# Mirroring more of a symmetric score matrix in a gated attention unit followed by a mixture of experts

## The chip, the cores and the metric

The kernel runs on one core of one Trainium2 chip. The metric is the device time of one execution in microseconds (us). Before the change it is 883.23 us, the median of three runs (883.2 to 883.38). Engines are called by their names or as the profile has them: PE is TensorE's matmuls, PEld its weight loads, DVE VectorE, ACT ScalarE, POOL GpSimd, SP SyncE, which here only issues DMAs.

## What is computed

The reference has two stages. With B = 8 sequences of S = 2816 rows, D = 256 and 64 columns of z:

```python
def _attn_ref(u, v, z):
    scores = (1.0 / S) * np.matmul(z, z.transpose(0, 2, 1))
    attn = np.maximum(scores, 0.0) ** 2
    out = np.matmul(attn, v)
    return u * out

def _moe_ref(x, w_gate, w1_dense, w2_dense, w1, w2):   # x: the 22528 rows of the first stage
    y_dense = np.maximum(x @ w1_dense, 0.0) @ w2_dense
    logits = x @ w_gate
    expert_idx = np.argmax(logits, axis=1)              # one of 8 experts for each row
    probs = softmax(logits)
    for e in range(8):
        rows = expert_idx == e
        y_moe[rows] = probs[rows, e][:, None] * (np.maximum(x[rows] @ w1[e], 0.0) @ w2[e])
    return y_dense + y_moe
```

Since the scores are z times its own transpose, each sequence's attention matrix is symmetric: the block of keys k and queries q is the transpose of the block of keys q and queries k.

## The kernel before

**Blocks and groups.** A sequence is cut into 22 blocks of 128 rows. The queries of a sequence are worked off in six groups of 2, 4, 4, 4, 4 and 4 blocks (line 268). For each group `n` there is a buffer `A[n]` in SBUF with the squared scores of all 22 key blocks against the group's query blocks, in bf16. There are three such buffers, so group `n` takes the buffer of group `n - 3`; `open_group` (line 353) hands it out.

**Scores.** One call of `scores` (line 375) issues two matmuls on the two halves of TensorE's rows (64 columns of z each; the turned z, `zT`, holds z twice) and fills one pair of PSUM banks with two key blocks by four query blocks, 1024 numbers a partition. `relu` (line 397) then offers two passes, each to ScalarE or VectorE (the second of the first two groups also to GpSimd): relu and scale from PSUM to `r` (lines 405 and 407), and the square from `r` to `A[n]` (lines 418 and 420).

**Mirrored scores before.** For a group two back in the same sequence (`far[n]`, line 346) the scores are not computed again: a DMA transpose on SP's queue (line 468, in `far_steps`) writes the blocks of `A[n - 2]`, turned, into `A[n]` where they would have been. So `left[n]`, the list of score calls still to be issued for a group, leaves those keys out. The four transposes of a sequence are put into a list `turning` when the group that they read begins, and each is issued at one of a few places inside the multiplication (line 586), when the plan holds the source to be complete.

**Products.** `av(n, i, between)` (line 553) multiplies two query blocks of a group with `v`: two passes over the 22 key blocks, on each half of the rows one matmul per key block (line 579), 88 matmuls in all into one pair of banks. In the first two blocks of a group the first pass takes the keys in the order in which the plan expects them (`key_at`). Between the matmuls `fill` (line 483) issues score calls of this group, the next, or the one after it (`ahead`, line 495), when a pair of banks is free. Between the two passes `swap_rows` (line 531) issues a tiny matmul (`touch`, line 527) and two score calls, or two touches if no score may be computed ahead.

**After the products.** `gate_x` (line 602) multiplies with u on VectorE (line 606), which frees the output banks, and has SP turn the result (`xT`, line 608) for the expert logits. u comes in on SP's queue (`load_u`, line 141) four blocks ahead. Then each block is routed, and its rows are scattered by expert into a table in DRAM (`scatter`, line 717, on GpSimd's queue).

**The order.** The order of TensorE, ScalarE, VectorE and SP is written out by the program while it is built. The planner keeps a clock `now`, times at which each engine is free, and estimates of durations; `offer` and `run` hand the passes to the engine that ends first. Work tied to a block is registered with `at` and `soon`: `soon(t, ...)` puts it on VectorE at block `t` (counted over all sequences). In this way z of the next sequence is loaded at block 0 of each sequence (`load_z`, line 103, GpSimd's queue), and turned at blocks 5 and 6 (`turn_z`, line 108: a VectorE copy that doubles z, line 113, and a DMA transpose on SP's queue, line 116). v of the next sequence is loaded in eight parts at blocks 13 to 18. The weights of the second stage go into `wall` (8 experts, 2048 columns each), three loads a sequence at blocks 15, 18 and 21, from sequence 1 on.

**Second stage.** When the attention is done, the rows come back by expert in tiles of 256 or 128 (`fetch`), are multiplied with the dense weights and the expert's (`up`, `down`, lines 936 and 944), and scattered to the output (line 962). The change does not touch it.

Of the kernel before, what the change touches and what calls it, by code (L numbers as in the profile page):

```python
# [15 lines left out]
P = 128  # L16
# [3 lines left out]
def kernel(  # L20
# [13 lines left out]
    B, S, D = u.shape  # L34
    dq = z.shape[2]
    E = moe_w_gate.shape[1]
    F = moe_w1_dense.shape[1]
    N = B * S
    assert D == 256 and dq == 64 and F == 512 and E == 8 and S % (2 * P) == 0
    nK = S // P  # L40
# [19 lines left out]
    WD = 2 * F + 4 * D  # L60
# [47 lines left out]
    def turn_z(b, k0, k1):  # L108

        if k0 == 0:  # L110
            zn_of[b] = zpool.tile([P, nK, 2, dq], BF, name="zn", bufs=1)
            zT_of[b] = zpool.tile([P, nK, P], BF, name="zT")
        nc.vector.tensor_copy(
            zn_of[b][:, k0:k1, :, :],
            z_of[b][:, k0:k1, :].unsqueeze(2).to_broadcast([P, k1 - k0, 2, dq]))
        nc.sync.dma_start_transpose(
            out=zT_of[b][:, k0:k1, :],
            in_=zn_of[b][:, k0:k1].rearrange("p k h d -> p (k h d)"))
        if k1 == nK:
            z_there.add(b)  # L120

# [11 lines left out]
    now = [0.0]  # L133
# [4 lines left out]

    z_of, zn_of, zT_of, v_of, ut_of, xT_of, lg_of, rs = {}, {}, {}, {}, {}, {}, {}, {}

    def load_u(g, gate=False):
        ut = aw.tile([P, 2, D], F32, name="ut", bufs=3)
        if gate:
            nc.vector.memset(ut[:, 0, 0:1], 0.0)
        b, i = divmod(g, nK)
        nc.sync.dma_start(out=ut[:], in_=uf[:, b, i:i + 2, :])
        ut_of[g] = ut[:]


# [114 lines left out]
    A = {}  # L264
    groups = []
# [75 lines left out]
        run(now[0])  # L341


    left, far, key_at = {}, {}, {}
    for n, (b, i0, w) in enumerate(groups):
        far[n] = [m for m in (n - 2,) if m >= 0
                  if groups[m][0] == b]
        turned = {k for m in far[n] for k in range(groups[m][1], groups[m][1] + groups[m][2])}
        ks = [k for k in range(0, nK, 2) if k not in turned]

        left[n] = [tuple(ks[x:x + 4 // w]) for x in range(0, len(ks), 4 // w)]
# [88 lines left out]
        ts = [key_at.get((m, k)) for k in range(i0, i0 + w)]  # L440
        return None if None in ts else max(ts)

    def turned_to(a, n):

        _, j0, wj = groups[a]
        w = groups[n][2]
        flat = A[n].rearrange("p k c -> p (k c)")
        return flat[:, j0 * w * P:(j0 + wj) * w * P]

    def block(n, k, c):  # L450

        _, i0, w = groups[n]
        for a in far[n]:
            _, j0, wj = groups[a]
            if j0 <= k < j0 + wj:
                x = c * wj + k - j0
                return turned_to(a, n)[:, x * P:(x + 1) * P]
        return A[n][:, k, c * P:(c + 1) * P]

    def far_steps(a):  # L460

        _, j0, wj = groups[a]

        def step(n):
            _, i0, w = groups[n]
            assert a + 1 in A
            open_group(n)
            nc.sync.dma_start_transpose(
                out=turned_to(a, n).rearrange("p (x c) -> p x c", c=P),
                in_=A[a][:, i0:i0 + w, :].rearrange("p k c -> p (k c)"))  # L470
            turn_at[0] = now[0] + 0.17 * w * wj
            read_at[a] = now[0] + 1.5 + 0.19 * w * wj
            for j in range(wj):
                key_at[n, j0 + j] = now[0] + 7.0

        return [(a, lambda n=n: step(n), n) for n in (a + 2,) if a in far.get(n, [])]

    turning = []
    turn_at = [0.0]
    read_at = {}  # L480
    jobs = []

# [70 lines left out]
    def av(n, i, between):  # L553
        b, i0, w = groups[n]
        if i == i0:
            turning.extend(far_steps(n))
        keep[0] = 0
        if n == 0 and i == i0:

            fill(n)  # L560
            need(n, 0)
        until(lambda: pairs[0][0] if pairs else None)
        ox = take_pair()
        o = banks(ox, "o")
        for p in range(2):
            rest = list(range(nK))
            for x in range(nK):
                k = rest[0]
                if i == i0 and p == 0:

                    k = min(rest, key=lambda k: (max(key_at.get((n, k), 9e9), v_at(n, k)), k))
                    need(n, k)
                rest.remove(k)
                if n == 0 and i == i0 and p == 0 and x in (12, 14, 16):
                    load_u(2 * (x - 12) // 2, gate=True)
                for h in range(2):
                    r = slice(h * dq, (h + 1) * dq)
                    j = p ^ h
                    nc.tensor.matmul(out=o[:, j, 0:D], lhsT=block(n, k, i + j - i0)[r],  # L579
                                     rhs=v_of[b][r, k, :], start=(p == 0 and x == 0),  # L580
                                     stop=(p == 1 and x == nK - 1))
                pe(0.1092)
                keep[0] = 2 - p if x >= nK - 12 else 0
                if x % 2 == 1 and x < nK - 1:
                    fill(n)
                if x in (3, 10, 17)[1 - p:] and turning and turn_at[0] <= now[0]:
                    t = can_turn(turning[0][2], turning[0][0])
                    if t is not None and t <= now[0] and turning[0][0] + 1 in A:
                        turning.pop(0)[1]()
            if p == 0:  # L590
                swap_rows(n)
                between()

        def done(t):
            give_pair(t + 0.1, ox)

        g = b * nK + i
        offer(now[0] + 0.2, 0, {"dve": (0.63, lambda eng: gate_x(g, o))}, done)
        keep[0] = 0


    def gate_x(g, o):
        g0 = g % (2 * G)
        x = pays[:, g0:g0 + 2, 0:D]
        assert g + 1 < 2 * G or (g - 2 * G in placed and g + 1 - 2 * G in placed)
        nc.vector.tensor_mul(x, o[:, :, 0:D], ut_of.pop(g))  # L606
        xT = aw.tile([P, 5, P], BF, name="xT", bufs=8)
        nc.sync.dma_start_transpose(
            out=xT[:], in_=pays[:, g0:g0 + 2, :].rearrange("p n r -> p (n r)")[:, 0:5 * P])
        for j in range(2):  # L610
            xT_of[g + j] = xT[:, 3 * j:3 * j + 2, :]

# [399 lines left out]
    def soon(t, fn, dur=0.07):  # L1012
        at(t, lambda: offer(now[0], 3, {"dve": (dur, lambda eng: fn())}))
# [7 lines left out]
    for b in range(B):  # L1021
        t = b * nK
        if b + 1 < B:
            soon(t, lambda b=b: load_z(b + 1))
            soon(t + 5, lambda b=b: turn_z(b + 1, 0, nK // 2), 0.4)
            soon(t + 6, lambda b=b: turn_z(b + 1, nK // 2, nK), 0.4)
            for h in range(8):
                soon(t + 13 + 5 * h // 7, lambda b=b, h=h: load_v(b + 1, h, 8))

    ts = [b * nK + x for b in range(1, B) for x in (15, 18, 21)][2:]  # L1030
    soon(ts.pop(0), lambda: dense(w1d, moe_w1_dense, 2))
    soon(ts.pop(0), lambda: dense(w2d, moe_w2_dense, 4))
    for e in range(E):
# [151 lines left out]
```

## Time and profile before

The page gives for one profiled execution the busy time of each engine. That execution took 883.35 us, its span from the first instruction to the last 881.2 us.

| | us, or share |
|---|---|
| median of three runs | 883.23 |
| profiled execution | 883.35, span 881.2 |
| TensorE matmuls busy | 861.5 (98%), 12257 instructions |
| TensorE weight loads busy | 757.7 (86%) |
| VectorE busy | 700.9 (80%) |
| ScalarE busy | 737.2 (84%) |
| GpSimd busy | 491.6 (56%) |
| matmuls with v (line 579) | 7744, busy 491.1 |
| score matmuls (line 390) | 944, busy 156.8 |
| DMA queue of SP | 70.23 MB, 46.2% of 16 engines |
| DMA queue of GpSimd | 55.45 MB, 29.6% of 16 engines |

Busy shares are means over the span. The attention ends near 555 us, where the matmuls of line 936 begin to follow each other; before that VectorE and ScalarE are busy above 80% in all slices but the first and the last two, after it between 30 and 80%. A row of a group of instructions reads: line, engine, operation, what is written and read, shapes, count, then busy time and the mean of one in ns, then the idle time of the engine before them and what ended it. In the chain of waits a row is the start, the length, and what held the end at that time.

### The profile page before, as it was taken

How to read it: one execution, taken by the hardware profiler on the slowest of the kernel's cores; microseconds unless marked ns; L12 is line 12 of the kernel's file. 1: busy time of each engine (PE TensorE's matmuls, PEld its weight loads, DVE VectorE, ACT ScalarE, POOL GpSimd, SP SyncE). 2: the span in 40 equal slices, each digit the busy share in tenths (PEclk: the TensorE clock that was granted, in tenths of full speed). 3: DMA queues.
4: the chain of work that ended last, by engine and by line, in shares of the span. 5: the costliest groups of instructions: out<-in, count | busy, mean ns of one | idle time of the engine just before them, and what ended most of it. 6: DMA issues, size and time to landing. Idle time of an engine off the chain costs nothing.

```text
span 881.2 us, 30493 instructions
## 1 busy us (share of the span) xinstructions
PE 861.5 (98%) x12257; PEld 757.7 (86%) x12257; DVE 700.9 (80%) x1348; ACT 737.2 (84%) x913; POOL 491.6 (56%) x560
## 2 busy tenths in 40 slices
PE   7999999999999999999999999999999999999995
PEld 5788898898888888888888888888888888889994
DVE  7999999998999999999999996756665445446663
ACT  7999998998998998998998994577777777777773
POOL 8203355445426436436336334588888888877664
PEclk9999999999999999999999999999999999999998
DMA  8897988979979979989999976465646565533442
GB/s 155 148 151 139 161 162 149 185 165 173 181 161 185 167 165 185 162 181 143 198 182 165 165 135 115 104 136 131 136 122 120 121 123 122 124 103 103 95 98 76
DMA packets 258830, 127.62 MB, mean 145 GB/s; under 512 B 222846, under 2 KB 237438, under 8 KB 258688
## 3 DMA queue, kind: packets, MB, share of 16 engines
q1 hardware_dynamic: 227040, 70.23, 46.2%
q0 software_dynamic: 31648, 55.45, 29.6%
q8 instruction: 96, 1.57, 0.8%
q14 instruction: 46, 0.38, 0.1%
HBM read 61.54 MB, written 37.16 MB: 112 GB/s over the span
## 4 chain that ended last, share of the span: by engine, by line
PE 81%; POOL 6%; issue 4%; DVE 4%; DMA 2%; ACT 1%; SPq 0%; POOLq 0%; DVEq 0%; ACTq 0%
PE o L579 44%; PE h_ps L936 13%; PE yy L944 12%; PE s L390 10%; POOL out_dram L962 5%; DMA out_dram<-ring,ix 1%; DVE r L407 1%; PE lg L634 1%; POOL A L420 1%; DVE A L420 1%; ACT r L405 1%; DMA ring<-xs 1%; DVE pays L606 0%; ACT A L418 0%; DMA z<-in_z_dram 0%
## 5 line engine op out<-in xcount | busy, mean ns | idle before, releaser
L579 PE MATMUL o<-vb,A 64*128 64x256 bf16 x7744 | 491.1, 269 | 3.3 <-POOL A L420 1.7
L579 PEld LDWEIGHTS <-A 64*128 64x128 bf16 x7744 | 406.5, 94 | 53.7 <-POOL A L420 3.0
L724 POOL DMA_INDIRECT xs<-pays,pi x176 | 190.2, 1081 | 249.3 <-DVE pi L722 204.5
L405 ACT ACTIVATE r<-s 128x1024 f32<-128x1024 f32 (+1 forms) x268 | 263.8, 1012 | 21.6 <-PE s L390 19.2
L418 ACT ACTIVATE A<-r 128x1024 bf16<-128x1024 f32 (+1 forms) x263 | 266.6, 1046 | 7.1 <-DVE r L407 4.2
L939 ACT ACTIVATE ring<-h_ps 128x1024 bf16<-128x1024 f32 x180 | 184.1, 1024 | 89.6 <-PE h_ps L936 88.1
L407 DVE TENSOR_SCALAR r<-s 128x1024 f32<-128x1024 f32 (+1 forms) x164 | 197.6, 1215 | 6.5 <-PE s L390 1.9
L420 DVE TENSOR_TENSOR A<-r 128x1024 bf16<-128x1024 f32 x161 | 196.4, 1231 | 2.1 <-ACT r L405 1.7
L960 DVE SCALAR_TENSOR_TENSOR ring<-yy,me,ring 128x256 f32<-128x256 f32 x180 | 86.9, 483 | 124.6 <-ACT ring L959 84.7
L962 POOL DMA_INDIRECT out_dram<-ring,me x140 | 147.5, 1054 | 42.0 <-issue 24.4
L390 PE MATMUL s<-zT 64*128 64x512 bf16 (+1 forms) x944 | 156.8, 357 | 1.8 <-ACT zT L192 0.6
L944 PEld LDWEIGHTS <-ring 128*128 128x128 bf16 x1440 | 140.1, 98 | 16.1 <-issue 0.3
L944 PE MATMUL yy<-w2d,ring 128*128 128x256 bf16 x720 | 108.0, 273 | 0.1
L944 PE MATMUL yy<-ring 128*128 128x256 bf16 x720 | 108.0, 273 | 0.0
L936 PE MATMUL h_ps<-ring,w1d 128*128 128x256 bf16 x720 | 93.3, 272 | 1.0 <-DVE pays L606 0.8
L936 PE MATMUL h_ps<-ring 128*128 128x256 bf16 (+1 forms) x880 | 93.7, 253 | 0.0
L924 DVE COPY ring<-wall 128x2048 bf16 x110 | 79.7, 740 | 8.0 <-DVE ring L960 4.0
L936 PEld LDWEIGHTS <-ring 128*128 128x128 bf16 x880 | 74.3, 98 | 6.8
L936 PEld LDWEIGHTS <-w1d 128*128 128x128 bf16 x720 | 70.1, 98 | 9.3 <-issue 1.0
L390 PEld LDWEIGHTS <-zT 64*128 64x128 bf16 x944 | 57.6, 94 | 16.5 <-issue 2.6
L606 DVE TENSOR_TENSOR pays<-o,ut 128x512 bf16<-128x512 f32 x88 | 60.4, 687 | 14.0 <-PE o L579 13.7
L959 ACT COPY ring<-yy 128x256 f32<-128x256 f32 x180 | 65.9, 366 | 1.8 <-PE yy L944 1.8
(120 smaller groups left out, 370.0 us busy)
## 6 DMA issues: line engine op xcount, KB each, us to landing
ut<-in_u_dram SPq DMA_DIRECT2D x88, 256.0 KB
vb<-in_v_dram POOLq DMA_DIRECT2D x42, 192.0 KB
wall<-in_moe_w_dram POOLq DMA_DIRECT2D x16, 256.0 KB
xs<-pays,pi POOLq DMA_INDIRECT x176
zr<-in_z_dram POOLq DMA_DIRECT2D x7, 352.0 KB
out_dram<-ring,me POOLq DMA_INDIRECT x140
ring<-xs SPq DMA_TRANSPOSE x114
vb<-in_v_dram POOLq DMA_DIRECT2D x14, 128.0 KB
```

The lines of the kernel that those rows point to most:

```text
L390: nc.tensor.matmul(out=s[:, h, y * c:(y + 1) * c], lhsT=zT[r, k + h, :], rhs=zT[r, i0:i0 + w, :], start=True, stop=True)
L405: nc.scalar.activation(r[:, :, :c], s[:, :, :c], AF.Relu, scale=1.0 / S)
L407: nc.vector.tensor_scalar(out=r[:, :, :c], in0=s[:, :, :c], scalar1=1.0 / S, scalar2=0.0, op0=ALU.mult, op1=ALU.max)
L418: nc.scalar.activation(a, r, AF.Square)
L420: (nc.gpsimd if eng == "pool" else nc.vector).tensor_mul(a, r, r)
L579: nc.tensor.matmul(out=o[:, j, 0:D], lhsT=block(n, k, i + j - i0)[r], rhs=v_of[b][r, k, :], start=(p == 0 and x == 0), stop=(p == 1 and x ...
L724: ins = nc.gpsimd.indirect_dma_start(out=xs, out_offset=bass.IndirectOffsetOnAxis(ap=pi[:], axis=0), in_=pays[:, g % (2 * G), 0:ROW].bitca ...
L936: nc.tensor.matmul(out=h_ps[:, f, hs, :], lhsT=w1(c, f), rhs=xT[:, hs, c, :], start=(c == 0), stop=(c == 1))
L939: nc.scalar.activation(h, h_ps[:].rearrange("p f h t -> p f (h t)"), AF.Relu)
L944: nc.tensor.matmul(out=y[:, k, :], lhsT=h[:, f, j * P:(j + 1) * P], rhs=w2(f), start=(f == 0), stop=(f == 3))
L960: nc.vector.scalar_tensor_tensor(out=ys, in0=y[:, 1, :], scalar=me[:, j, 0:1], in1=yd, op0=ALU.mult, op1=ALU.add)
L962: ins = nc.gpsimd.indirect_dma_start(out=out, out_offset=bass.IndirectOffsetOnAxis(ap=ids[j], axis=0), in_=ys, in_offset=None, bounds_chec ...
```

## The change

All pairs of groups in the same sequence that lie two or more apart are mirrored, where before only those exactly two apart were. The pairs three to five apart have no room in `A`, so their turned blocks go into `wall`, which is empty until the weights come: `mirror` gives each pair, by the numbers of the two groups in their sequence, its place. `slots(b)` says which of them exist: all six in sequences 0 to 5, two in sequence 6, none in sequence 7. `block` returns the place from which a product reads.

`far_steps(a)` makes one transpose for each target group; where there are four targets, the last two share one. For a group of four blocks the step for group `a + 2`, which needs a new buffer, comes last. The planner gets a clock of SP's queue, `sync`, that every transpose and every u load moves forward (0.18 us a block, 0.6, 1.25 and 1.5), and a step is issued when this clock is within 0.5 us of now. Mirrored keys are expected 3.0 us after their place on that clock (before: 7.0 us after the issue), and the source counts as read 3.5 us after it; scores of the group that takes the source's buffer wait for that in `ahead`.

z is moved: that of sequence `b + 1` is loaded at block 13 of sequence `b - 1` and turned at blocks 19 and 20 of it (sequence 1 keeps blocks 0, 5 and 6 of sequence 0). An assertion at build time makes sure that no score of the sequence whose turned z is overwritten is left by then. The weight loads move to blocks 20 and 21 of sequences 1 to 5, five places in sequence 6 and blocks 0, 5, 10 and 15 of sequence 7.

```diff
@@ -108,6 +108,7 @@
     def turn_z(b, k0, k1):
 
         if k0 == 0:
+            assert not any(left[m] for m in left if groups[m][0] == b - 2)
             zn_of[b] = zpool.tile([P, nK, 2, dq], BF, name="zn", bufs=1)
             zT_of[b] = zpool.tile([P, nK, P], BF, name="zT")
         nc.vector.tensor_copy(
@@ -116,6 +117,7 @@
         nc.sync.dma_start_transpose(
             out=zT_of[b][:, k0:k1, :],
             in_=zn_of[b][:, k0:k1].rearrange("p k h d -> p (k h d)"))
+        issue(1.5)
         if k1 == nK:
             z_there.add(b)
 
@@ -138,12 +140,18 @@
 
     z_of, zn_of, zT_of, v_of, ut_of, xT_of, lg_of, rs = {}, {}, {}, {}, {}, {}, {}, {}
 
+    sync = [0.0]
+
+    def issue(dur, ready=0.0):
+        sync[0] = max(sync[0], now[0], ready) + dur
+
     def load_u(g, gate=False):
         ut = aw.tile([P, 2, D], F32, name="ut", bufs=3)
         if gate:
             nc.vector.memset(ut[:, 0, 0:1], 0.0)
         b, i = divmod(g, nK)
         nc.sync.dma_start(out=ut[:], in_=uf[:, b, i:i + 2, :])
+        issue(0.6)
         ut_of[g] = ut[:]
 
 
@@ -341,10 +349,20 @@
         run(now[0])
 
 
+    spare = wall[:].rearrange("p e w -> p (e w)")
+    mirror = {(2, 5): (E - 1) * WD, (1, 5): (E - 2) * WD, (1, 4): (E - 3) * WD,
+              (0, 4): (E - 4) * WD, (0, 5): (E - 4) * WD + 8 * P, (0, 3): (E - 5) * WD + 2 * F}
+
+    def slots(b):
+
+        if b < B - 2:
+            return list(mirror)
+        return [(2, 5), (1, 5)] if b == B - 2 else []
+
     left, far, key_at = {}, {}, {}
     for n, (b, i0, w) in enumerate(groups):
-        far[n] = [m for m in (n - 2,) if m >= 0
-                  if groups[m][0] == b]
+        far[n] = [m for m in range(max(n - 5, 0), n - 1)
+                  if groups[m][0] == b and (m == n - 2 or (m % 6, n % 6) in slots(b))]
         turned = {k for m in far[n] for k in range(groups[m][1], groups[m][1] + groups[m][2])}
         ks = [k for k in range(0, nK, 2) if k not in turned]
 
@@ -440,43 +458,52 @@
         ts = [key_at.get((m, k)) for k in range(i0, i0 + w)]
         return None if None in ts else max(ts)
 
-    def turned_to(a, n):
+    def turned_to(a, n, w):
 
         _, j0, wj = groups[a]
+        if a == n - 2:
+            flat = A[n].rearrange("p k c -> p (k c)")
+            return flat[:, j0 * w * P:(j0 + wj) * w * P]
+        x = mirror[a % 6, n % 6]
+        return spare[:, x:x + w * wj * P]
+
+    def block(n, k, c):
+
         w = groups[n][2]
-        flat = A[n].rearrange("p k c -> p (k c)")
-        return flat[:, j0 * w * P:(j0 + wj) * w * P]
-
-    def block(n, k, c):
-
-        _, i0, w = groups[n]
         for a in far[n]:
             _, j0, wj = groups[a]
             if j0 <= k < j0 + wj:
                 x = c * wj + k - j0
-                return turned_to(a, n)[:, x * P:(x + 1) * P]
+                return turned_to(a, n, w)[:, x * P:(x + 1) * P]
         return A[n][:, k, c * P:(c + 1) * P]
 
     def far_steps(a):
 
         _, j0, wj = groups[a]
 
-        def step(n):
-            _, i0, w = groups[n]
-            assert a + 1 in A
-            open_group(n)
+        def step(ns):
+            n = ns[0]
+            i0, w = groups[n][1], sum(groups[m][2] for m in ns)
+            if n == a + 2:
+                open_group(a + 1)
+                open_group(n)
             nc.sync.dma_start_transpose(
-                out=turned_to(a, n).rearrange("p (x c) -> p x c", c=P),
+                out=turned_to(a, n, w).rearrange("p (x c) -> p x c", c=P),
                 in_=A[a][:, i0:i0 + w, :].rearrange("p k c -> p (k c)"))
-            turn_at[0] = now[0] + 0.17 * w * wj
-            read_at[a] = now[0] + 1.5 + 0.19 * w * wj
-            for j in range(wj):
-                key_at[n, j0 + j] = now[0] + 7.0
-
-        return [(a, lambda n=n: step(n), n) for n in (a + 2,) if a in far.get(n, [])]
+            issue(0.18 * w * wj, read_at.get(a - 1, 0.0) if n == a + 2 else 0.0)
+            read_at[a] = sync[0] + 3.5
+            for m in ns:
+                for j in range(wj):
+                    key_at[m, j0 + j] = sync[0] + 3.0
+
+        ns = [[n] for n in range(a + 2, min(a + 6, len(groups))) if a in far[n]]
+        if len(ns) == 4:
+            ns[2:] = [ns[2] + ns[3]]
+        elif groups[a][2] == 4:
+            ns = ns[1:] + ns[:1]
+        return [(a, lambda m=m: step(m), m[-1]) for m in ns]
 
     turning = []
-    turn_at = [0.0]
     read_at = {}
     jobs = []
 
@@ -583,9 +610,9 @@
                 keep[0] = 2 - p if x >= nK - 12 else 0
                 if x % 2 == 1 and x < nK - 1:
                     fill(n)
-                if x in (3, 10, 17)[1 - p:] and turning and turn_at[0] <= now[0]:
+                if x in (3, 10, 17)[1 - p:] and turning and sync[0] <= now[0] + 0.5:
                     t = can_turn(turning[0][2], turning[0][0])
-                    if t is not None and t <= now[0] and turning[0][0] + 1 in A:
+                    if t is not None and t <= now[0]:
                         turning.pop(0)[1]()
             if p == 0:
                 swap_rows(n)
@@ -607,6 +634,7 @@
         xT = aw.tile([P, 5, P], BF, name="xT", bufs=8)
         nc.sync.dma_start_transpose(
             out=xT[:], in_=pays[:, g0:g0 + 2, :].rearrange("p n r -> p (n r)")[:, 0:5 * P])
+        issue(1.25)
         for j in range(2):
             xT_of[g + j] = xT[:, 3 * j:3 * j + 2, :]
 
@@ -1021,13 +1049,16 @@
     for b in range(B):
         t = b * nK
         if b + 1 < B:
-            soon(t, lambda b=b: load_z(b + 1))
-            soon(t + 5, lambda b=b: turn_z(b + 1, 0, nK // 2), 0.4)
-            soon(t + 6, lambda b=b: turn_z(b + 1, nK // 2, nK), 0.4)
+            soon(max(t - 9, 0), lambda b=b: load_z(b + 1))
+            soon(t - 3 if b else 5, lambda b=b: turn_z(b + 1, 0, nK // 2), 0.4)
+            soon(t - 2 if b else 6, lambda b=b: turn_z(b + 1, nK // 2, nK), 0.4)
             for h in range(8):
                 soon(t + 13 + 5 * h // 7, lambda b=b, h=h: load_v(b + 1, h, 8))
 
-    ts = [b * nK + x for b in range(1, B) for x in (15, 18, 21)][2:]
+    ts = [b * nK + x for b in range(1, B - 2) for x in (20, 21)][1:]
+    ts += [(B - 2) * nK + x for x in (14, 16, 18, 20, 21)]
+    ts += [(B - 1) * nK + x for x in (0, 5, 10, 15)]
+    assert len(ts) == 2 + 2 * E
     soon(ts.pop(0), lambda: dense(w1d, moe_w1_dense, 2))
     soon(ts.pop(0), lambda: dense(w2d, moe_w2_dense, 4))
     for e in range(E):
```

## The prediction

> **What bounds the kernel now.** I read the busy times by stretch first, then the chain of waits inside one sequence, then the groups of instructions. A stretch row gives its bounds and length, then each engine's busy microseconds (and instructions), the granted clock, the DMA share and GB/s.
>
> ```profile
> span 881.2 us, 30493 instructions
> ...
> 20.00:87.00 67.00, 65.33 (x1077) 56.21 (x1074) 64.79 (x99) 64.69 (x71) 16.05 (x23) 1.00 0.84 145
> 221.00:288.00 67.00, 66.91 (x1143) 58.41 (x1139) 63.63 (x119) 63.09 (x69) 29.80 (x34) 1.00 0.92 173
> 489.00:556.00 67.00, 64.69 (x1107) 55.70 (x1102) 56.74 (x134) 47.60 (x53) 26.97 (x26) 1.00 0.76 133
> 620.00:881.00 261.00, 251.12 (x2456) 226.54 (x2453) 141.75 (x290) 184.22 (x289) 198.82 (x228) 0.99 0.49 112
> ```
>
> ```profile
> 222.10 1.25 SPq L468 DMA_TRANSPOSE A<-A  x1
> ...
> 288.89 1.29 SPq L468 DMA_TRANSPOSE A<-A  x1
> ```
>
> The first mirror transpose of two neighbouring sequences starts 66.8 us apart, so a stretch of 67 us is one sequence: TensorE (first) is busy 66.91 us of it. VectorE (63.63) and ScalarE (63.09) are nearly full too, so a TensorE that only waits in turn for them has to be excluded. The chain does that; the first row is the chain from 200 to 300 us.
>
> ```profile
> by line: PE o L579 79.2%; PE s L390 17.9%; PE lg L634 1.9%; PE d L527 0.4%; PE pre L664 0.4%; PE pre L665 0.1%; issue 0.1%
> ...
> 206.47 0.22 PE s L390 x2
> 206.69 0.66 PE o L579 x12
> 207.34 0.22 PE s L390 x2
> ```
>
> The chain never leaves TensorE: 79% products with v, 18% scores. A score call of the code is two matmuls and takes 0.22 us of that chain. So from the second sequence on a score call left out shortens the kernel by its TensorE time, provided nothing else becomes late; the ScalarE and VectorE time that it frees brings nothing of its own.
>
> The Trainium skill (Perfetto Trace Analysis, "Identifying the Most-Contended Engine") holds that matmul busy time is a poor measure of TensorE's headroom and that the busy share of weight loads is to be read: here 58.41 of 67 us, 87%. By that rule TensorE may be less full than 66.91 makes it look; the chain with 0.1% issue disagrees, and I go by the chain.
>
> **Scores removed.**
>
> ```profile
> L390 PE MATMUL s<-zT 64*128 64x512 bf16 x768 | 140.1, 376 | 1.1 <-ACT r L405 0.4 <-DVE ut L144 0.2 <-DVE r L407 0.2
> ...
> L390 PE MATMUL s<-zT 64*128 64x256 bf16 x176 | 16.7, 270 | 0.7 <-ACT zT L192 0.6
> L405 ACT ACTIVATE r<-s 128x1024 f32<-128x1024 f32 x261 | 259.7, 1024 | 21.6 <-PE s L390 19.2 <-POOL A L420 0.7 <-DVE A L420 0.7
> L407 DVE TENSOR_SCALAR r<-s 128x1024 f32<-128x1024 f32 x163 | 197.0, 1218 | 6.5 <-PE s L390 1.9 <-POOL A L420 1.6 <-ACT A L418 1.3
> L418 ACT ACTIVATE A<-r 128x1024 bf16<-128x1024 f32 x256 | 262.2, 1057 | 7.0 <-DVE r L407 4.2 <-DVE wall L253 2.3
> L420 DVE TENSOR_TENSOR A<-r 128x1024 bf16<-128x1024 f32 x161 | 196.4, 1231 | 2.1 <-ACT r L405 1.7
> ```
>
> A call covers two key blocks by four query blocks. Groups 0 to 5 of a sequence need 6, 11, 10, 9, 9, 9 calls now, 54. With every group two or more back mirrored, group 3 needs 8 (group 0's two keys fall away), group 4 needs 6, group 5 needs 4: 45. That holds for sequences 0 to 5; sequence 6 keeps the pairs (2,5) and (1,5), 4 calls fewer; sequence 7 is as before. Together 6 x 9 + 4 = 58 calls, 116 matmuls of 944. At 0.22 us: **12.8 us less TensorE**. ScalarE and VectorE lose 58 x 2 passes of 1.0 to 1.2 us, about 130 us of engine time, which leaves the path only where they bind: in the stretch from 20 to 87 TensorE idles 1.67 us, in that from 489 to 556 2.31. Of these 4.0 us I take nothing (most of the last belongs to sequence 7, which keeps its scores); they are the lower bound of the sum.
>
> **Swaps that find no score.** Between the two passes of every two query blocks the code puts a touch and two scores on TensorE, or, when no score may be computed ahead, two touches.
>
> ```profile
> 233.24 0.50 PE s L390 x4
> ...
> 136.02 0.05 PE d L527
> 136.07 0.04 issue
> 136.12 0.16 PE d L527
> ...
> L527 PE MATMUL d<-ones 64*128 64x8 bf16 x97 | 16.1, 166 | 0.8
> ```
>
> With scores the swap costs 0.50 - 2 x 0.22 = 0.06 us beyond them, without 0.25: 0.19 more. 97 touches for 88 swaps mean 9 empty ones now. Fewer scores make more. ScalarE and VectorE have room for some 55 calls in 67 us (two passes of 1.1 us on two engines, less VectorE's other work), 9 to 10 in the 12 us of a four-block group. While groups 0 to 5 are multiplied, the scores of the group two ahead become free: 10, 8, 6, 4, 6, 11. Groups 3 and 4 run dry before their second swap; that is two empty swaps a sequence where there is one. I take one more in each of six sequences: **+1.2 us**; bounds 0 and four more in each (24 x 0.19 = 4.6).
>
> **Mirrors added.** They go on the SP queue, in order with the u loads (ut) and the transposes of x (xT).
>
> ```profile
> xT<-pays SPq DMA_TRANSPOSE x88
> ...
> A<-A SPq DMA_TRANSPOSE x32
> ...
> zT<-zn SPq DMA_TRANSPOSE x14
> ```
>
> ```profile
> 16.00:18.00 2.00, 2.00 (x36) 1.77 (x34) 1.99 (x2) 2.00 (x3) 1.27 (x2) 1.00 0.97 328
> 509.90:513.00 3.10, 3.10 (x54) 2.40 (x52) 2.82 (x10) 2.83 (x4) 0.97 (x1) 1.00 1.11 202
> 390.00:422.00 32.00, 31.91 (x552) 28.22 (x551) 29.86 (x61) 29.48 (x33) 16.69 (x21) 1.00 1.10 159
> 221.00:256.00 35.00, 35.00 (x590) 29.95 (x586) 34.01 (x58) 33.59 (x36) 12.77 (x13) 1.00 0.93 176
> ```
>
> In blocks of 128 x 128 bf16 (32.8 KB) a sequence transposes 56 mirrored, 55 for x and 22 for z. The six pairs add 8+8+8+16+16+16 = 72, in five more transposes (groups 4 and 5 of group 0 share one): 32 issues become 6 x 9 + 6 + 4 = 64. The second row is nearly all transposes, at 202 GB/s: 0.16 us a block, 11.7 us more a sequence. The first row is u loads alone, at 328. The third has almost the same share as the second with a fifth fewer bytes, so the share counts packets that wait and is no measure of work; I go by bytes. The 11.57 MB of a sequence (173 GB/s x 67 us) hold 133 blocks, 4.36 MB. Afterwards 6.72 MB at 202 and 6.95 MB at 328 (one 0.26 MB weight load fewer) take 33.3 + 21.2 = 54.5 us, 84% of 65. The dense part is 221 to 256: 6.17 MB now; z's 22 blocks leave it and the 72 come, 158 blocks, 5.18 MB, 25.6 + 7.2 = 32.8 us of 34. It fits, barely; the rest of the sequence has room. So the mirrors lie beside TensorE at **no cost of their own**, but with little cover left.
>
> A group two back is read at the earliest one whole group after its mirror is issued, the deeper ones later, and the first pass of a group takes its keys in the order in which they are expected. What a late one costs has one neighbouring row, a v part that came late:
>
> ```profile
> PE o L579 <- DMA vb<-in_v_dram: 0.5, 1, 0.5
> ```
>
> I take one such wait in all, **+0.6 us**; bounds 0 and one in each of seven sequences, 3.5.
>
> **The wait and the moves.** Far scores now wait until all mirrors of the group whose buffer they take are issued and, by the plan, read. It holds back TensorE fills, not the products; with VectorE and ScalarE freed the later start is made up. What a mirror's own wait blocks is SP's queue:
>
> ```profile
> SPq L468 <- ACT r L405: 35.0, 13, 5.9
> SPq L146 <- DVE pays L606: 48.9, 15, 5.6
> ...
> 227.29 5.45 SPq L468 DMA_TRANSPOSE A<-A  x1
> ...
> 509.30 1.77 SPq L468 DMA_TRANSPOSE A<-A  x1
> ```
>
> Sixteen blocks hold SP for 1.77 us on a quiet queue and 5.45 on a full one. Behind them stand ut and xT; VectorE's gate (L606) needs ut and frees the output bank. ut is ordered four blocks ahead, about 12 us, and twice 5.45 fits into that. Cost 0; without this cover it is the slow rival below.
>
> z moves from blocks 0, 5, 6 to 13, 19, 20 of the sequence before: a clear and a load (POOL's queue, among the v loads), two VectorE copies and two transposes.
>
> ```profile
> L113 DVE COPY zn<-zr 128x1408 bf16<-128x1408 bf16 x14 | 12.2, 872 | 0.0
> ...
> L253 DVE MEMSET wall<- x16: 59/59/59, 211.1 to 544.2; 128x1 bf16 x16
> ...
> L924 DVE COPY ring<-wall x110: 681/695/1140, 551.0 to 864.9; 128x2048 bf16 x110
> ```
>
> The copies are the same 0.87 us, the z has six blocks (18 us) to arrive, and its transposes wait on TensorE scores that lie a sequence back. The weights come later, the last at block 15 of sequence 7 instead of 18, before the first use at 551.0. Both: 0.
>
> **Sum.** -12.8 + 1.2 + 0.6 = -11.0. Span 881.2 becomes 870.2; the profiled run took 883.35, 2.15 more than its span and 0.12 above the median, so the median of 883.23 becomes **872.2**.
>
> **The rivals.**
> A, the forecast; its own range is 867.5 (4.0 us of idle time and no empty swap) to 876.
> B, the plan runs dry: four empty swaps a sequence (4.6) and a late mirror in each of seven (3.5): -12.8 + 8.1 = -4.7, 878.5. For it: one empty swap a sequence already with full engines. Against it: the far scores need not be early.
> C, slower: DMA paces blocks 0 to 11. It holds if the share is work: 0.93 x 35 = 32.6, plus 50 blocks of 0.18 (0.16 x 1.11) is 41.6, less 0.8 for the weight load, 40.8; at a top of 1.11 that takes 36.8 us. ut comes late, the gate keeps the bank, TensorE stands: 1.8 us a sequence over today, six times, +11, 894. It decides from a top below 40.8/35 = 1.17; above that the stage ends sooner than now. For it: 1.10 over 32 us is the most that a long stretch shows. Against it: those 32 us had TensorE at 31.91. The Trainium skill (DMA: Bandwidth & Descriptors, "Issuing engines are not separate DMA queues") says that transfers started by SP and POOL interleave on the same 16 engines; the trace agrees in that both shares add up past 1. It speaks for C.
> D, no gain: TensorE only looks full and the pace is that of a plan whose banks come free at ScalarE's and VectorE's speed; the places of the scores become waits: 883. For it: both at 94%. Against it: the chain, and both get faster.
>
> **How the numbers follow.** A 0.55, B 0.22, C 0.14, D 0.07, other 0.02. Below 0.2% (1.8 us) a measurement of this kernel tells no change. Faster: A and B and a little, 0.78; same: D and the edge of B, 0.08; slower 0.14. The range runs from 867.5, A's lower bound, to 883.5, which takes in B and D and leaves out C.
>
> **What would show it.** L390 x828; L405 and L407 together 374 instead of 432; 64 mirror transposes; TensorE near 65 us between the first mirrors of neighbouring sequences; some 103 touches, no wait of L579 on A<-A over 0.6 us. Wrong: TensorE idle over 1 us in a middle sequence, waits of L606 on ut or of L390 on a bank (C), over 120 touches (B), or 67 us a sequence with a busy, unwaiting TensorE (D).

## The result and the profile after

The changed kernel takes 892.81 us (median of 4 runs, 891.79 to 896.13) against 883.31: 1.0112 of before, interval 1.0084 to 1.0139. It is slower by 9.5 us where 11 us less were forecast. The changed kernel's page, of the execution that took 896.13 us, has these rows:

```profile
span 894.2 us, 30214 instructions
...
PE 858.3 (96%) x12165; PEld 747.4 (84%) x12165; DVE 655.4 (73%) x1308; ACT 671.9 (75%) x837; POOL 501.1 (56%) x560
...
L408 PE MATMUL s<-zT 64*128 64x512 bf16 (+1 forms) x828 | 138.0, 357 | 15.1 <-ACT r L423 11.9
```

The score matmuls are 828, as counted, and VectorE and ScalarE lose 45 and 65 us. TensorE lost its even flow. By stretch (length, PE, PEld, DVE, ACT, POOL, clock, DMA share, GB/s):

```profile
87.00:154.00 67.00, 66.62 (x1155) 57.48 (x1152) 57.49 (x111) 53.46 (x59) 31.82 (x31) 1.00 1.12 198
...
288.00:355.00 67.00, 63.67 (x1073) 54.34 (x1070) 53.55 (x100) 49.04 (x54) 31.05 (x33) 0.97 1.14 191
...
422.00:489.00 67.00, 66.91 (x1155) 58.58 (x1151) 60.15 (x116) 59.30 (x64) 30.61 (x34) 1.00 1.06 181
```

Six pairs are mirrored in sequences 0 to 5. The first row is mostly sequence 1: TensorE is busy 66.62 of 67 us at 198 GB/s, so six pairs alone do not starve it. In sequences 2 to 5 (154 to 422 us) it idles 2.4 to 3.8 us in 67, at 191 to 201 GB/s. The last row, mostly sequence 6 with two pairs, is full again. A sequence has eleven pairs of query blocks, one in group 0 and two in each of groups 1 to 5. The time from the first product of each pair to that of the next, worked out from the traces, in sequence 3 (with two kernels of the experiments below):

```text
                g0    g1    g1    g2    g2    g3    g3    g4    g4    g5    g5    sum
before         6.15  5.93  6.69  6.23  5.92  5.72  6.31  5.94  6.46  6.35  5.72  67.4
after          5.93  5.93  7.41  5.60  5.73 10.08  5.52  6.04  5.84  6.67  5.72  70.5
no_dma_again   5.93  6.15  6.69  6.01  5.71  5.72  5.09  6.04  6.13  6.14  5.93  65.6
no_u           5.93  5.93  7.49  5.59  5.73  5.73  5.52  6.04  5.84  6.68  5.72  66.2
```

Most pairs take about as long as before or less; one, the first of group 3, loses 4.4 us. It is the same pair in sequences 3, 4 and 5. In sequence 0 the first pair of group 4 loses 5.5 us and in sequence 2 the second pair of group 4 loses 3.1, where TensorE itself waits 2.0 us for a transpose of x (`xT`). Sequence 1 takes 66.0 us without a stall, sequences 2 to 5 take 69.6 to 70.9. The chain through that place in sequence 4 (start, length, what held the end):

```profile
318.82 2.31 PE o L606 x40
...
321.94 7.07 DMA A<-A
...
329.08 2.00 ACT A L436 x2
331.09 0.92 ACT r L423
...
332.05 0.38 PE s L408 x2
332.43 3.24 PE o L606 x40
```

The mirror that reads group 1's buffer needs 7.07 us from its issue. Group 4's scores take that buffer, and ScalarE, in order, stands before the first square that writes it. Behind it stands the relu that would free a pair of banks; TensorE's next score has none. Then 40 products take 3.24 us where they took 2.31 at 318.82. The granted clock, the third number from the end in the stretches around it, is lower there. Above the stretches stands the gap itself, here and in sequence 5, and below them the stretch after the gap in sequence 5:

```profile
332.05 0.39 PE L408 MATMUL s<-zT 64*128 64x512 bf16 x2 [2.37 <-ACT r L423]
...
403.44 0.39 PE L408 MATMUL s<-zT 64*128 64x512 bf16 x2 [2.38 <-ACT r L423]
...
328.00:332.00 4.00, 1.68 (x31) 1.25 (x26) 1.63 (x3) 2.92 (x4) 0.97 (x1) 1.00 0.96 220
332.00:336.00 4.00, 3.95 (x47) 2.97 (x48) 2.42 (x3) 2.94 (x3) 0.97 (x1) 0.68 1.05 224
336.00:340.00 4.00, 4.00 (x64) 3.20 (x62) 3.51 (x6) 2.73 (x3) 1.03 (x2) 0.90 1.22 174
...
403.00:407.00 4.00, 3.56 (x61) 2.96 (x62) 3.13 (x4) 3.34 (x4) 0.97 (x1) 1.00 1.08 228
```

So in sequence 4 the pair loses 3.9 us: its gap of 2.4 us and about 1.5 us more at the lower clock. In sequence 5 the same gap is not followed by a lower clock; there TensorE itself has waited 1.06 us for a mirror just before, and the pair loses 3.7 us. The Trainium skill (TensorE: Matmul & The Clock Gate, "Part 1: The HAM clock gate") describes a gate on this clock, which halves it after an idle window of about 3.4 us. The trace agrees in part: gaps of 2.41 and 2.37 us in sequences 3 and 4 were enough, one of 2.38 us in sequence 5 was not, and what decides between them is open. The waits of that execution (who for whom: total, times, longest):

```profile
ACT A L436 <- DMA A<-A: 21.1, 8, 6.4
...
PE s L408 <- ACT r L423: 11.9, 8, 3.3
```

### The profile page after: what moved, and what is told of

It reads as the page before. It is cut to its first block, busy times and chain, and to the rows that moved or that the text cites. A ratio compares the mean times of both kernels' runs of the same rounds, so it can differ in the third digit from the quotient of the medians.

```text
span 894.2 us, 30214 instructions
## 1 busy us (share of the span) xinstructions
PE 858.3 (96%) x12165; PEld 747.4 (84%) x12165; DVE 655.4 (73%) x1308; ACT 671.9 (75%) x837; POOL 501.1 (56%) x560
## 2 busy tenths in 40 slices
DMA packets 319246, 142.83 MB, mean 160 GB/s; under 512 B 283262, under 2 KB 297854, under 8 KB 319104
## 4 chain that ended last, share of the span: by engine, by line
PE 63%; DMA 12%; issue 9%; POOL 8%; DVE 4%; ACT 2%; SPq 0%; POOLq 0%; DVEq 0%; ACTq 0%
PE o L606 31%; PE h_ps L964 13%; PE yy L972 13%; PE s L408 6%; POOL out_dram L990 5%; DMA A<-A 4%; DMA zr<-in_z_dram 3%; DMA xs<-pays,pi 2%; DMA vb<-in_v_dram 2%; DVE r L425 2%; DMA out_dram<-ring,ix 1%; ACT r L423 1%; POOL xs L752 1%; ACT A L436 1%; DMA wall<-A 1%
## 5 line engine op out<-in xcount | busy, mean ns | idle before, releaser
L606 PE MATMUL o<-vb,A 64*128 64x256 bf16 x6816 | 436.8, 272 | 4.8 <-DMA vb<-in_v_dram 1.8
L606 PEld LDWEIGHTS <-A 64*128 64x128 bf16 x6816 | 352.2, 95 | 55.1 <-issue 4.3
L752 POOL DMA_INDIRECT xs<-pays,pi x176 | 198.4, 1127 | 259.0 <-DVE pi L750 197.2
L423 ACT ACTIVATE r<-s 128x1024 f32<-128x1024 f32 (+1 forms) x227 | 223.4, 1013 | 67.9 <-PE s L408 65.1
L436 ACT ACTIVATE A<-r 128x1024 bf16<-128x1024 f32 x228 | 233.9, 1054 | 33.4 <-DMA A<-A 21.1
L425 DVE TENSOR_SCALAR r<-s 128x1024 f32<-128x1024 f32 (+1 forms) x147 | 176.4, 1210 | 24.6 <-PE s L408 21.8
L438 DVE TENSOR_TENSOR A<-r 128x1024 bf16<-128x1024 f32 (+1 forms) x138 | 165.0, 1205 | 17.9 <-ACT r L423 10.6
L408 PE MATMUL s<-zT 64*128 64x512 bf16 (+1 forms) x828 | 138.0, 357 | 15.1 <-ACT r L423 11.9
L408 PEld LDWEIGHTS <-zT 64*128 64x128 bf16 x828 | 50.8, 94 | 28.3 <-issue 17.9
L606 PE MATMUL o<-vb,wall 64*128 64x256 bf16 x928 | 71.7, 272 | 0.0
```

Source lines behind the costliest of these rows:

```text
L408: nc.tensor.matmul(out=s[:, h, y * c:(y + 1) * c], lhsT=zT[r, k + h, :], rhs=zT[r, i0:i0 + w, :], start=True, stop=True)
L423: nc.scalar.activation(r[:, :, :c], s[:, :, :c], AF.Relu, scale=1.0 / S)
L425: nc.vector.tensor_scalar(out=r[:, :, :c], in0=s[:, :, :c], scalar1=1.0 / S, scalar2=0.0, op0=ALU.mult, op1=ALU.max)
L436: nc.scalar.activation(a, r, AF.Square)
L438: (nc.gpsimd if eng == "pool" else nc.vector).tensor_mul(a, r, r)
L752: ins = nc.gpsimd.indirect_dma_start(out=xs, out_offset=bass.IndirectOffsetOnAxis(ap=pi[:], axis=0), in_=pays[:, g % (2 * G), 0:ROW].bitca ...
```

## The experiments

Three theories, the second in two forms. T1: one read is planned too early, whatever the load. T2: the DMAs can't carry what the change adds, either over the whole sequence or in its first half, where the mirrors are ("local"). T3: the plan runs dry of scores. A ratio is to the kernel before on the same chip, with a 95% interval; below 1 is faster.

**First four, on a slower chip.** There the kernel before takes 922.57 us, and the second stage, which the change leaves alone, 357 to 361 us instead of 327, so that these four were read for direction and repeated (v with the plan unchanged). The changed kernel as it is was not run on that chip.

A later planned read, so that the scores that take the buffer are ordered later:

```diff
-            read_at[a] = sync[0] + 3.5
+            read_at[a] = sync[0] + 8.0
```

> The changed kernel with one number changed: the plan takes a group's buffer as read by its mirrors 8.0 us after their place on SP's clock, not 3.5, so the scores that overwrite the buffer are ordered later. Theory T1 (one late read): in sequences 2 to 5 ScalarE stands some 3 us before a score that overwrites a buffer that a mirror transpose is still reading, TensorE runs out of score banks for 2.5 us and then works at a lower granted clock; ordered later, that wait and the 4 us in one pair of query blocks a sequence go, and the kernel comes to 872 to 880. Rival T2 (DMA capacity): the transfers of a sequence do not fit beside 65 us of TensorE, a later order only moves the wait: 888 to 895.

1.0192 (1.0129 to 1.0254): no gain.

Weights behind the mirrors:

```diff
-    ts = [b * nK + x for b in range(1, B - 2) for x in (20, 21)][1:]
+    ts = [b * nK + x for b in range(1, B - 2) for x in (12, 13)][1:]
```

> The changed kernel with the weight loads of sequences 1 to 5 at blocks 12 and 13 instead of 20 and 21, behind the mirrors instead of just ahead of them. T1 in the form that the weights at the end of a sequence push the next sequence's mirrors late: the 4 us stalls of sequences 2 to 5 shrink or go, 876 to 886, the stall of sequence 0 stays. T2: the same bytes, no gain, 889 to 895.

1.007 (1.0032 to 1.0108): slower than before; whether it is less slow than the changed kernel can't be said on this chip.

The 58 score calls left out as in the changed kernel, and the transposes that replace them left out too. The products read the turned block of the pair two apart, and the plan expects the keys at other times, so that the order differs somewhat:

```diff
-                return turned_to(a, n, w)[:, x * P:(x + 1) * P]
+                return turned_to(n - 2, n, w)[:, x * P:(x + 1) * P]
...
         def step(ns):
             n = ns[0]
+            if n != a + 2:
+                return
...
-            for m in ns:
-                for j in range(wj):
-                    key_at[m, j0 + j] = sync[0] + 3.0
+            for m in far[n]:
+                for j in range(groups[m][2]):
+                    key_at[n, groups[m][1] + j] = sync[0] + 3.0
```

> The changed kernel without the transposes of the pairs three to five apart; their products read the turned block of the pair two apart in their place, so the values are wrong, but TensorE, ScalarE and VectorE have the same work. Both T1 and T2: with 72 blocks a sequence fewer on the queue the stalls go, 870 to 874, which is the gain of the 58 score calls alone. Rival T3 (the plan itself runs dry of scores, whatever DMA does): 880 or more.

0.9854 (0.9784 to 0.9925). T3 falls: without the added transposes the same 58 calls fewer bring a gain.

No v after the first sequence:

```diff
-                soon(t + 13 + 5 * h // 7, lambda b=b, h=h: load_v(b + 1, h, 8))
+                pass
...
-                                     rhs=v_of[b][r, k, :], start=(p == 0 and x == 0),
+                                     rhs=v_of[0][r, k, :], start=(p == 0 and x == 0),
```

> The changed kernel that loads v of the first sequence only and multiplies all sequences with it: about 2.9 MB a sequence fewer on GpSimd's queue at blocks 13 to 18. T2 (capacity over the whole sequence): 15% of the DMA work goes, 874 to 882. T1 (a wait at one place, the first block pairs after the mirrors, blocks 9 to 11): the v loads are not there at that time, 887 to 893.

1.0109 (1.0076 to 1.0142): no gain.

**The dose, on a chip on which the kernel before takes 883.92 us.** The kernels before and after as they are, and two and three of the six pairs (three are shown; two leave (1,4) out as well):

```diff
-    mirror = {(2, 5): (E - 1) * WD, (1, 5): (E - 2) * WD, (1, 4): (E - 3) * WD,
-              (0, 4): (E - 4) * WD, (0, 5): (E - 4) * WD + 8 * P, (0, 3): (E - 5) * WD + 2 * F}
+    mirror = {(2, 5): (E - 1) * WD, (1, 5): (E - 2) * WD, (1, 4): (E - 3) * WD}
```

> The kernel before, for its trace on the chip on which the next three run. No theory expects a difference from the kernel before: ratio 1.00.

> The changed kernel as it is, on the same chip. All theories: slower by about 1%, 1.008 to 1.015 of before.

> The changed kernel with two of the six pairs, (2,5) and (1,5), in sequences 0 to 6: 4 score calls (0.9 us of TensorE) and 32 blocks more to turn a sequence instead of 9 and 72. T2 in its local form (SP's queue can't turn 128 blocks in the first half of a sequence): with 88 blocks it can, the stalls go and the kernel gains 6.2 us less an empty swap a sequence, 0.993 to 0.997 of before. T1 (one read planned too early by the changed estimates, whatever the load): the stall stays, 1.000 to 1.015.

> The changed kernel with three pairs, (2,5), (1,5) and (1,4): 6 calls and 48 blocks more a sequence (two pairs in sequence 6). T2, local: between the two, 0.990 if 104 blocks still fit, 1.00 to 1.005 if they do not; the place of a stall would be the group after group 1. T1: 1.000 to 1.015 as with two.

One run of before: 883.88. After: 1.0098 (1.0069 to 1.0128). Two pairs: 0.9959 (0.9936 to 0.9982). **Three pairs: 0.9909 (0.9887 to 0.9932), 876.64 us, faster than both kernels.** T1 falls: with the same estimates and fewer blocks the stalls are gone. Two stretches of three pairs:

```profile
221.00:288.00 67.00, 66.82 (x1152) 58.34 (x1150) 59.31 (x115) 57.42 (x63) 33.25 (x33) 1.00 1.13 195
288.00:355.00 67.00, 66.41 (x1144) 57.99 (x1140) 58.45 (x116) 56.76 (x63) 33.30 (x33) 1.00 1.22 193
```

TensorE is full at 193 to 195 GB/s, about the rate at which six pairs starve it. Three pairs bring 11.57 - 0.26 + 48 x 0.0328 = 12.9 MB a sequence, at 195 GB/s 66.1 us (66.2 measured; this is no test, since the rate is these bytes over this time). Six bring 13.67 MB, at the same rate 70.1 us: sequences 2 to 5 of the changed kernel take 69.6 to 70.9. That fits a ceiling of some 195 GB/s, but does not show one; the next runs speak against it as the whole cause.

**What is to be taken away.** Without u, the plan unchanged:

```diff
+    ut_first = []
+
     def load_u(g, gate=False):
+        if g >= 6:
+            issue(0.6)
+            ut_of[g] = ut_first[g // 2 % 3]
+            return
...
+        ut_first.append(ut[:])
```

> The changed kernel that loads three u tiles and gates all blocks with them: 2.9 MB a sequence fewer on SP's queue, spread evenly, so about 1.5 MB of it in the first half of a sequence, where the mirrors are; the plan of all other work is unchanged, so the values are wrong but the work is the same. T2, local (SP's queue and the DMA engines can't do the first half's transfers in its 33 us): the stalls of groups 3 and 4 shrink or go, 0.985 to 0.998 of before. T1 (a wait planned wrongly whatever the load): 1.005 to 1.015.

Without v, the plan now unchanged too (the planner's time for GpSimd is kept, the load left out):

> The changed kernel that loads v of the first sequence only and multiplies all sequences with it, the plan unchanged: as many bytes fewer from memory as without u, but on GpSimd's queue at blocks 13 to 18, behind the mirrors. T2, local: the stall at blocks 9 to 11 stays, 1.005 to 1.015. T2 over the whole sequence: 0.985 to 0.998, as without u.

> The kernel of the earlier run without the transposes of the pairs three to five apart, now beside the others on a chip on which the kernel before takes 883 us: the value of the 58 score calls alone, 0.984 to 0.989 of before (870 to 874).

> The kernel of the earlier run with the longer planned read time (8.0 us), on a chip on which the kernel before takes 883 us. T2: 1.00 to 1.02, the wait is spread over other block pairs or moved; T1: 0.985 to 0.997.

Without u (no_u): 0.9906 (0.989 to 0.9923), 874.47 us; of ScalarE's 21.1 us of waits on mirrors one of 1.8 us is left. Without v (no_v): 1.016 (1.0127 to 1.0193). Without the added transposes (no_dma_again): 0.9881 (0.9857 to 0.9904). With the longer planned wait (wait8_again): 1.0145 (1.0067 to 1.0222). u and v are as many bytes in memory, but u comes on SP's queue, evenly, and v behind the mirrors. Two cautions go with the pair. The DMAs of the profile move 22.3 MB less without u and only 10.1 MB less without v (142.83 MB with both). And leaving u out takes its loads off the queue on which the mirrors wait in order, so that less load and a shorter queue are not told apart. What no_v does show by itself is that the mean over a sequence does not decide: its sequence 5, whose second stall is at 394 us, moves 12.2 MB, less than three pairs do without a stall, and takes 74.2 us. In two parts:

```profile
357.00:392.00 35.00, 32.47 (x553) 27.48 (x551) 29.37 (x54) 24.64 (x27) 13.59 (x12) 1.00 1.18 181
392.00:431.00 39.00, 35.99 (x583) 29.75 (x581) 27.30 (x51) 27.90 (x31) 12.82 (x13) 0.91 0.68 151
```

The room that the v loads leave is in the second part, after the stall. Why no_v is slower than the changed kernel itself is not explained. The longer planned wait only moves the wait. Its rows:

```profile
PE o L606 <- DMA vb<-in_v_dram: 4.9, 2, 4.2
...
PE o L606 <- DMA A<-A: 4.7, 3, 2.9
...
ACT A L436 <- DMA A<-A: 3.1, 2, 2.2
```

ScalarE waits 3.1 us instead of 21.1, and TensorE now waits itself, for v and for mirrors that come late.

**What was left open: number or place, and the transposes alone.** Group 0's three pairs alone (`mirror` with (0,4), (0,5), (0,3), none in sequence 6); all but (0,3); and all six transposed but not used:

```diff
-        turned = {k for m in far[n] for k in range(groups[m][1], groups[m][1] + groups[m][2])}
+        turned = {k for m in far[n] if m == n - 2 for k in range(groups[m][1], groups[m][1] + groups[m][2])}
...
-        for a in far[n]:
+        for a in [a for a in far[n] if a == n - 2]:
...
-            for m in ns:
+            for m in [m for m in ns if m == a + 2]:
```

> The changed kernel with the three pairs of group 0 alone, (0,3), (0,4) and (0,5), in sequences 0 to 5: 3 calls and 24 blocks a sequence. If the number of blocks decides: no stall, 18 calls or 3.9 us less an empty swap a sequence, 0.994 to 0.998 of before. If group 0's place ahead of group 1 on the queue decides: a stall at groups 3 or 4 as with all six, 1.000 to 1.012.

> The changed kernel without the pair (0,3): five pairs, 8 calls and 64 blocks a sequence. If the number of blocks decides: between three pairs (0.991, 48 blocks) and six (1.010, 72 blocks), 0.993 to 1.005, with stalls shorter than with six. If the place decides: 1.005 to 1.010, stalls of 4 us as with six.

> The changed kernel with all six pairs transposed but not used: the scores of these groups are computed as before, 432 calls, and the products read them. DMA capacity: the 72 blocks cost their time without the scores' gain, and ScalarE and VectorE, full again, can't catch up after a stall: 1.02 to 1.04 of before. If the transposes lay beside TensorE as the prediction had it: 0.998 to 1.004.

> The kernel of the earlier run with the weight loads of sequences 1 to 5 at blocks 12 and 13, beside the others. If the 0.5 MB a sequence just ahead of the mirrors take part in the stall: 0.990 to 1.004. If they do not: 1.005 to 1.013.

Five pairs: 1.0031 (0.9989 to 1.0072), between three and six; 13.4 MB at 195 GB/s would be 68.8 us, and sequences 2 to 5 take 67.2 to 69.4. The transposes alone: 1.0162 (1.0093 to 1.0231), below the 1.02 that was expected, but far from nothing. The weights moved: 1.0045 (1.0026 to 1.0063), a gain in part: the first pair of group 3 is back at 5.71 us in sequences 3 to 5, but groups 4 and 5, where the weights now come, lose 2 to 3 us there and 6 us in sequence 2.

Group 0's pairs alone: 1.0048 (1.003 to 1.0065), against the number, which is only 24 blocks. The pairs that stall are the first of group 2 in sequences 3 and 5 and the second of group 1 in sequence 4. In sequences 3 and 5 ScalarE again stands before a square until mirrors have been read (8.1 and 8.2 us from their issue). In sequence 4 the chain runs over another DMA:

```profile
286.96 0.79 POOL wall L267
...
290.45 0.39 POOL wall L263
...
291.52 8.95 DMA xs<-pays,pi
...
300.67 0.10 DVE pays L632
```

A scatter, issued on GpSimd's queue behind two weight loads, takes 8.95 us; VectorE's gate waits to overwrite the rows it reads. So there is not one place but one crowded time, from the end of a sequence to its tenth block: z's transposes and the weights, then the mirrors, u and xT; who waits depends on what is queued behind what.

The traces say one thing more about the pair that stalls most. Group 1's mirror for group 3 is the second mirror of a sequence before the change and the sixth after it. Its rows on SP's queue in sequence 4, where group 3 begins at 326.67:

```profile
316.40 3.47 SPq L490 DMA_TRANSPOSE wall<-A  x1
319.97 0.54 SPq L153 DMA_DIRECT2D ut<-in_u_dram  x1
320.60 1.29 SPq L635 DMA_TRANSPOSE xT<-pays  x1
321.94 2.58 SPq L490 DMA_TRANSPOSE A<-A  x1
```

How long before group 3's first product it is issued, and then how long group 3's first pair takes, in us, in sequences 1 to 5:

```text
before         21.4  6.15   21.0  5.93   21.8  5.72   20.5  5.72   21.4  5.72
p3_pairs       12.4  5.93   13.6  5.93   11.7  5.93   10.7  5.93   10.5  5.93
no_u            8.7  5.73    8.4  5.73    7.2  5.73    8.1  5.73    8.0  5.73
weights_again   6.8  5.73    6.2  6.00    6.3  5.71    6.0  5.71    5.4  5.71
after           6.5  5.73    6.2  6.04    4.6 10.08    4.7  9.62    3.9  9.46
after_again     5.8  6.12    4.9  6.85    4.1  9.82    3.4 10.48    3.9  9.43
no_v            5.9  5.97    6.4  5.82    5.4  6.95    4.6  9.45    4.1 11.61
```

Against the 5.73 us of no_u, a mirror issued 6 us or more ahead costs at most some 0.4 us, one issued 4.9 to 5.9 us ahead up to 1.2, and one issued 4.7 us ahead or less 3.7 or more. So this stall goes with the time at which the mirror gets its turn on SP's queue, behind five other mirrors. The weights take part: they come on GpSimd's queue at the end of each sequence from sequence 1 on, and with them moved (weights_again) the mirror is issued earlier again. Whether SP is held longer because the DMA engines are busy or because more stands ahead in the queue was not separated. The stall of sequence 0 is open: weights_again has the same order of work there and does not stall.

## Why the prediction was wrong

**What bounds the kernel** was right: TensorE's flow. 58 calls fewer, without their transposes, bring 10.5 us (0.9881; interval 8.5 to 12.6) with 10 touches more than before, 107; with 0.19 us for each of these it is 12.4 us against 12.8 worked out.

**Empty swaps** were under-counted: 121 touches, 24 more and not 6, four a sequence as in case B. At 0.19 us that is 4.6 us instead of 1.2, a term of the sum that was mis-sized. With it the sum is 883.2 - 12.8 + 4.6 = 875.0; no_u, which has the same 121 touches and almost no wait on a mirror, takes 874.47. A slip besides: A's lower bound, with 4.0 us of idle time and no empty swap, comes to 867.0 and not 867.5.

**The step that failed** is "It fits, barely; the rest of the sequence has room. So the mirrors lie beside TensorE at no cost of their own", and with it the cost of 0 for what a mirror's wait on SP's queue holds up. The transfers cost 18 us: 892.81 against the 874.47 of no_u, and the added transposes alone, with all scores kept, cost 1.6% (1.0162). The sum added times of each kind alone, 202 GB/s for transposes and 328 for all loads, as if a mixture ran at their mean of some 250 GB/s (13.67 MB in 54.5 us). The stretches with six pairs show 191 to 201, those with three pairs 189 to 196, and stalls come even at 172 to 177 (no_v); so that neither 250 nor any mean rate tells whether a mirror is in time. For the pair that stalls most the turn on the queue tells it: group 1's mirror was issued 21 us ahead before the change, 4 to 7 after it. And the room in the second half is of no use to a mirror, since its source buffer is taken again three groups later.

The lost time came over that buffer, the cover that "Far scores now wait" took for granted: "It holds back TensorE fills, not the products". The order holds back the issue by the plan's times, but once a square is ordered, it stands in ScalarE's queue until the mirror has really been read, and with it every bank that ScalarE would free.

**Case C** gave 894 with a chance of 0.14; 892.81 was measured. That is luck in good part. Its thought, that the DMA work of a sequence's first half decides, was nearer to the truth than the sum by bytes for which it was put back. But its path was not found: no wait of the gate on u shows. Nor was its top of the share: three pairs show a share of 1.22 over 67 us with TensorE at 66.41, above the 1.17 from which C would have cost nothing, and no_v stalls at shares of 0.97 to 1.02.

**Late mirrors** (0.6 us) cost 1.1 us on TensorE itself, as small as taken. The moved z was not tested by itself. The moved weights take part in the crowded start, as weights_again shows, where they were put at 0. **Case D** is excluded by no_dma_again, where the scores left out bring their gain, and with it the doubt about matmul busy time: TensorE was as full as it looked.

## What to carry to other kernels

A transfer that replaces work is free only if it lands by its deadline, and bytes over a whole sequence do not tell that: here a sequence with 12.2 MB stalled and one with 12.9 MB did not. Find in the trace when the transfer is issued, what stands ahead of it on its queue, and when its source or target is taken next; here 21 us between issue and need became 4 to 7. Where both resources are near full, try a part of the exchange: here three pairs of six gain 0.9%, six lose 1%. Look for engines that work in order and wait for a DMA: here everything behind ScalarE's wait, banks that were long filled too, waited with it, and 3.1 us of it cost TensorE 3.9.

## What the runs showed of the hardware

A gap of 2.37 us on TensorE was followed by a granted clock of 0.68 over 4 us, another of 2.38 us by 1.00. The DMAs of this core moved a mixture of transposes, loads and scatters at 191 to 201 GB/s over 67 us in sequences 1 to 5 of the changed kernel; before, u loads alone ran at 328 over 2 us and a stretch that was nearly all transposes at 202 over 3.1 us. SP held 1.77 us for a transpose of 16 blocks on a quiet queue; in the changed kernel two of 8 and 16 blocks hold it for:

```profile
301.16 8.48 SPq L490 DMA_TRANSPOSE wall<-A  x2
```

One chip ran the kernel before in 922.57 us where three others took 883 to 884; in the four kernels traced there the second stage is 30 to 34 us longer.
